# A fused retention, dense and routed-expert kernel: scalings, routing copy and squares moved around the column read, and the order of the last dense units and first expert runs written out

## The chip, the cores and the metric

One core of a Trainium2 chip runs the kernel. The metric is the device time of one execution in microseconds. Five engines work side by side, each through its own queue: TensorE (PE in the profile, its weight loads PEld), VectorE (DVE), ScalarE (ACT), GpSimd (POOL) and SyncE (SP), which here only issues DMAs.

## What is computed

Three layers follow each other on 4608 tokens of 512 values.

```python
# 1: retention, 8 heads of 64, decay per head, sequences of 576
ret = scale * (q @ k^T) * Dmat ;  x = ret @ v
# 2: a dense layer, d_ff = 2048
h = x @ w_in ;  g = h - tanh(h) ;  x1 = g @ w_out
# 3: eight experts, top-1 routing by cosine logits of x1
gate, e = softmax / argmax(x1_normed @ emb_normed^T / tau)
out = gate * (relu(x1 @ w1[e]) @ w2[e])
```

## The kernel before

**Tiles and stages.** The tokens are 36 blocks of 128 (retention) and 18 groups of 256 (dense layer). A dense unit is one group with one eighth of d_ff: 144 units, numbered 0 to 143 in the order `seq`. Every 32-bit product is split in a high and a low part, so `mm1` (L480) has 24 matmuls of 256 columns and `mm2` (L548) 12 of 512. Between them one unit goes through `ch_a` (two ACT steps on the PSUM result h), `ch_c` (two ACT steps), `ch_u` (two DVE steps, the first of them, L518, frees h), `ch_e` (one ACT step, L527), `ch_f` (two DVE steps, L531 and L532, the second waits for L527), `ch_g` (the high part, ACT) and `ch_k` (the low part, DVE, L546). The h tiles have two PSUM buffers.

**Retention of one block.** `att_load` brings q, k, v, n (SP). `scale_q` and `scale_v` (L333, L337) scale q and v on DVE, in place. `b_pe` and `d_pe` (PE) form scores and state updates, `d_ev` and `b_ev` read them on DVE. `c_inter` (PE) puts the part that comes from earlier states in P, for one half of the array; `c_fence` (L432) then reads one column of P on DVE, and only behind that read may `c_pe` (PE) add the rest into the same P. `c_hi` and `c_lo` read P out as x. This read is called the column read.

**Routing of one group**, once its eight units are done: `r1_copy` copies x1 from PSUM (x1p) on DVE, `r1_sq` forms the squares on ACT, `r1_out` stores x1 (SP), `r1_norm` takes the root on POOL; then four small steps `route_2` to `route_5` find expert, gate and place, and `r5_out` writes them in a table in DRAM by indirect DMA (POOL). x1p has two PSUM buffers, both in use by one group.

**Experts.** A run is one expert with two or three tiles of 128 table rows. `b_rec` (L869) reads table rows (SP), `b_gather` (L877) fetches x1 of these tokens (POOL), `b_tr_pe` transposes (PE, L898), `b_tr_hi`/`b_tr_lo` split. `load_w` (L833) brings an eighth of an expert's weights (SP, two buffers of tag "ret"), `split_hi` and `split_lo` split it. `b_mm1`, `b_hi`, `b_lo`, `b_mm2` compute, `b_out` scatters.

**Order.** The schedule is manual: what is emitted first stands first in its engine's queue. Three texts follow each other: START (units 0 to 31 with the retention of blocks 0 to 9 and the splitting of the dense weights, which come as 64-bit words), the loop of `step` (units 32 to 135), and TURN (units 136 to 143 with the first two expert runs, each of two tiles). After them the loop of `b_step` runs the other experts. Before TURN, `early_shift`, `b_rec(0)` and `b_rec(1)` are emitted.

The letters in the texts, each with a number of a unit, block, group, weight piece or run: M `mm1`, N `mm2`, a c u e f g k the steps `ch_`; lq lk lv ln loads, sq sv scalings, B b D d `b_pe` to `d_ev`, I F C `c_inter`, `c_fence`, `c_pe`, xh xl `c_hi`, `c_lo`; R1a copy, R1b squares, R1c store, R1p norm, R2p to R5p the routing's PE steps, R2e to R5e, R2f and R5a its others, R5i the table write; L r R p o q h l the dense weights' load and splitting; W `load_w`, X Y its split, Z `b_rec`, G gather, T U V transposes and their split, P E H Q O the steps of an expert run. A ".V" or ".A" puts the step on DVE or ACT.

In `step(pos)` the block's steps come once in four units (pos % 4 == 2), `route_1` once in eight (pos % 8 == 2), the scalings at pos % 4 == 1, the loads at pos % 4 == 3. So every second column read meets a routing copy.

Of the kernel before, what the change touches and what calls it, by code (L numbers as in the profile page):

```python
# [34 lines left out]
M.136 M.137 a.136 c.136 a.137 c.137 W.0 e.135 f.135 X.0.V Y.0 G.4 G.5 G.0 G.1 u.136 W.1 W.2 X.1.V M.138 g.135 a.138  # L35
c.138 M.139 u.137 Y.1 k.135 N.134 W.3 e.136 f.136 N.135 X.2 Y.2 e.137 X.3 Y.3 f.137 g.137 k.137 g.136 k.136 a.139
c.139 M.140 u.138 R1a.16 R2p.16 M.141 R1b.16 a.140 c.140 u.139 W.4 W.5 e.139 X.4.V Y.4 e.138 f.138 g.138 k.138 u.140
X.5 T.4 f.139 M.142 R2e.16 R3p.16 R3e.16 W.6 N.136 a.141 c.141 R1c.16 R1p.16 e.140 Y.5 X.6 f.140 u.141 R4p.16 g.139
M.143 a.142 c.142 u.142 Y.6 e.142 N.137 N.138 W.7 T.0 W.8 X.8.V X.7 k.139 N.139 Y.7 a.143 c.143 g.140 f.142 g.142
u.143 R2f.16 e.141 Y.8 k.140 N.140 f.141 g.141 W.9 X.9 k.141 k.142 U.0 W.10 Y.9 N.141 W.11 T.1 X.10 Y.10 R4e.16  # L40
R5p.16 e.143 R5a.16 U.1 f.143 g.143 k.143 W.12 V.0 V.1 R5e.16 R5i.16 X.11.V Y.11 N.142 N.143 R1a.17 X.12 U.4 P.0 P.1
E.0 H.0 R2p.17 T.5 P.2 V.4 R1b.17 R1c.17 R1p.17 R2e.17 R3p.17 R3e.17 U.5 Q.0 E.2 H.2 Y.12 R4p.17 W.13 W.14 E.1 H.1
P.3 P.4 R2f.17 R4e.17 R5a.17 E.3.V X.13.V R5p.17 R5e.17 R5i.17 Y.13 H.3 Q.1 Q.2 W.15 Z.2 G.8 E.4 H.4 P.5 P.6 E.6.V
H.6 Q.3 Q.4 E.5.V H.5 P.7 Q.5 V.5 P.8 E.8 H.8 X.15 E.7.V H.7 Q.6 P.9 P.10 E.9.V H.9 P.11 G.9 Q.7 Q.8 Y.15 E.11 H.11
# [11 lines left out]
h.9 f.1 L.11 h.6 l.9 a.2 l.6 g.1 h.7 k.1 a.3 u.2 c.2 u.3 M.4 p.11 d.4 l.7 e.2 c.3 o.10 M.5 b.4 a.4 f.2 e.3 N.1 c.4  # L56
f.3 g.2 u.4 g.3 r.11 k.3 M.6 e.4 k.2 p.10 o.11 a.5 f.4 N.2 a.6 q.11 c.5 u.6 N.3 h.11 u.5 c.6 q.10 e.5 M.7 o.8 h.10
f.5 e.6 g.4 M.8 l.10 g.5 k.4 q.8 a.7 N.4 k.5 h.8 L.13 f.6 a.8 l.8 g.6 N.5 c.8 u.8 c.7 k.6 u.7 M.9 e.8 p.13 f.8 e.7
eg.0 N.6 g.8 l.11 a.9 f.7 r.13 M.10 u.9 g.7 c.9 k.7 k.8 e.9 o.13 N.7 a.10 f.9 c.10 u.10 I.4 g.9 M.11 F.4 e.10 q.13
f.10 h.13 C.4 a.11 l.13 M.12 lq.5 g.10 L.12 u.11 L.14 c.11 lv.5 k.10 N.8 e.11 k.9 a.12 sq.5 f.11 c.12 M.13 u.12 g.11  # L60
r.12 p.12.V k.11 e.12 N.9 o.12 a.13 f.12 c.13 M.14 u.13 p.14 r.14 sv.5 q.12 e.13 M.15 xh.4 o.14 h.12 xl.4 g.12 q.14
B.5 l.12 h.14 D.5 lk.6 lv.6 d.5 N.10 L.15 l.14 b.5 N.11 f.13 k.12 g.13.V I.5 a.14 sv.6 N.12 F.5 r.15 k.13 u.14 p.15
C.5 c.14 o.15 N.13 lq.6 q.15 xh.5 lk.8 e.14 xl.5 h.15 f.14 M.16 a.15 sq.6 g.14 u.15 c.15 B.6 l.15 M.17 e.15 lq.7
k.14 f.15 a.16 N.14 c.16 u.16 g.15.V e.16 sq.7 M.18 k.15 f.16 a.17 R1a.0 c.17 D.6 N.15 u.17 lk.7 g.16 R1c.0 R1b.0
d.6 e.17 R1p.0 M.19 R1a.1.A k.16 R2f.0 a.18 b.6 R1c.1 f.17 R1b.1 R2p.1 N.16 u.18 c.18 R1p.1 g.17.V R2f.1 R2e.1 k.17
R2p.0 e.18 I.6 a.19 f.18 N.17 R2e.0 F.6 u.19 c.19 B.7 g.18 C.6 lv.7 e.19 k.18 M.20 lq.8 f.19 xh.6 za.0 lk.9 xl.6
g.19 sv.7 N.18 k.19 sq.8 a.20 zb.0 c.20 D.7 u.20 zc.0 R3p.0 lv.8 R3p.1 d.7 e.20 N.19 R3e.1 b.7 sv.8 R4p.1 f.20 M.21
R4e.1 g.20 k.20 R5a.1 I.7 a.21 R3e.0 M.22 F.7 c.21 u.21 e.21 N.20 a.22 f.21 c.22 u.22 R4p.0 C.7 g.21.V e.22 R4e.0
M.23 xh.7 lq.10 ln.8 k.21 R5a.0 xl.7 f.22 N.21 a.23 sq.10 g.22 u.23 c.23 R5p.0 B.8 k.22 e.23 M.24 R5e.0 ln.9 f.23
R5i.0 D.8 a.24 N.22 d.8 lv.9 g.23 u.24 c.24 k.23 I.8 e.24 b.8 N.23 f.24 sv.9 g.24 F.8 R5p.1 k.24 M.25 R1a.2 R5e.1  # L70
R1b.2 R1c.2 C.8 M.26 a.25 R5i.1 lq.9 lk.10 xh.8 u.25 c.25 R1p.2 xl.8 R2p.2 a.26 sq.9 M.27 R2f.2 R2e.2 u.26 e.25 c.26
R3p.2 f.25 M.28 e.26 R3e.2 g.25.V f.26 R4p.2 k.25 g.26 B.9 R4e.2 a.27 N.24 ln.10 k.26 c.27 u.27 R5a.2 a.28 R5p.2 D.9
R5e.2 M.29 lv.11 e.27 c.28 u.28 R5i.2 d.9 e.28 N.25 f.28 f.27 I.9 N.26 g.28.V g.27 F.9 k.28 k.27 b.9 a.29 M.30 c.29
u.29 e.29 B.10 a.30 N.27 f.29 lv.10 c.30 u.30 g.29 M.31 e.30 sv.10 k.29 f.30 D.10 a.31 N.28 d.10 lk.11 g.30 c.31
# [1143 lines left out]
```

## Time and profile before

| | us |
|---|---|
| median of three runs | 1516.23 |
| lowest, highest | 1512.62, 1518.34 |
| the profiled execution | 1515.88 |
| its span in the trace | 1514.1 |
| PE busy in the span | 1428.7 (94%) |
| DVE busy | 955.8 (63%) |
| ACT busy | 777.2 (51%) |

The span is what the trace shows from the first instruction to the last. Busy time of PE is the time with at least one matmul under way; ends of matmuls are modelled, so neighbouring groups overlap a little. "Idle before" is the time an engine stood still, with the engine and tile that ended it.

### The profile page before, as it was taken

Reading aid. Unit: us, or ns where it says so; the run is one execution under the profiler, and the core shown is the slowest. Engines: PE = TensorE matmul, PEld = TensorE weight load, DVE = VectorE, ACT = ScalarE, POOL = GpSimd, SP = SyncE. Lnnn points to the kernel's source line nnn. Section 1 sums busy time; section 2 is a strip of 40 time slices with the busy share of each in tenths; the row PEclk is TensorE's granted clock in tenths of the full one; section 3 lists DMA queues with packets and bytes.
Section 4 is the critical chain, followed back from the end, with each engine's and each line's share of the span. In section 5 each row is a group of like instructions: output and inputs, shape, how many; then the busy total and the mean of one; then the engine's idle time right before and its main releaser. Section 6 shows DMA issues by size and latency. Waiting matters only on the chain. (4 is left out here: it accounts for less than half of the span.)

```text
span 1514.1 us, 30499 instructions
## 1 busy us (share of the span) xinstructions
PE 1428.7 (94%) x12696; PEld 1281.9 (85%) x12696; DVE 955.8 (63%) x1910; ACT 777.2 (51%) x1364; POOL 141.5 (9%) x140
## 2 busy tenths in 40 slices
...
GB/s 354 155 28 127 82 57 43 43 98 29 70 43 31 69 43 71 30 43 71 29 69 45 38 62 15 69 99 112 80 121 72 155 96 104 146 81 124 120 42 33
DMA packets 69517, 121.25 MB, mean 80 GB/s; under 512 B 9714, under 2 KB 26482, under 8 KB 69378
## 3 DMA queue, kind: packets, MB, share of 16 engines
...
## 5 line engine op out<-in xcount | busy, mean ns | idle before, releaser
L491 PEld LDWEIGHTS h<-x,w_i 128*128 128x128 f32 x3456 | 426.4, 192 | 32.1 <-issue 15.2
L491 PE MATMUL h<-x,w_i 128*128 128x256 f32 x3456 | 433.4, 282 | 19.2 <-DVE w L518 16.8
L561 PE MATMUL x1p<-w_o,g 128*128 128x512 f32 x1728 | 433.1, 400 | 1.7 <-ACT g L178 1.0
L561 PEld LDWEIGHTS x1p<-w_o,g 128*128 128x128 f32 x1728 | 317.0, 190 | 73.7 <-issue 6.2
L928 PE MATMUL bh<-bx,e 128*128 128x256 f32 (+1 forms) x1536 | 241.9, 307 | 0.8 <-DVE bg L948 0.8
L928 PEld LDWEIGHTS bh<-bx,e 128*128 128x128 f32 x1536 | 231.6, 188 | 10.8 <-DVE bg L948 1.2
L962 PE MATMUL bo<-e,bg 128*128 128x512 f32 x912 | 231.5, 396 | 0.0
L508 ACT ACTIVATE w<-h 128x512 f32<-128x512 f32 x144 | 85.8, 596 | 278.3 <-PE h L491 274.3
L948 DVE SCALAR_TENSOR_TENSOR bg<-bh,bg 128x384 fp32r<-128x384 f32 (+1 forms) x120 | 59.3, 495 | 238.8 <-ACT bg L942 228.8
L942 ACT ACTIVATE bg<-bh 128x384 fp32r<-128x384 f32 (+1 forms) x114 | 50.5, 444 | 286.6 <-PE bh L928 263.4
L962 PEld LDWEIGHTS bo<-e,bg 128*128 128x128 f32 x912 | 165.5, 188 | 29.1 <-issue 0.4
L518 DVE TENSOR_TENSOR w<-h,w 128x512 f32<-128x512 f32 x144 | 99.3, 690 | 115.7 <-ACT w L509 113.2
L532 DVE COPY_PREDICATED w<-w 128x512 f32<-128x512 int32 x144 | 109.0, 757 | 35.7 <-ACT w L527 22.6
L546 DVE TENSOR_TENSOR g<-w,g 128x512 fp32r<-128x512 f32 x144 | 98.9, 690 | 46.0 <-ACT g L178 46.0
L514 ACT ACTIVATE w<-w,nbias 128x512 f32<-128x512 f32 x144 | 104.3, 725 | 4.7
L724 POOL DMA_INDIRECT table<-rec,posi x36 | 45.4, 1260 | 656.3 <-DVE acc L718 601.6
L527 ACT ACTIVATE w<-w,nbias 128x512 f32<-128x512 f32 x144 | 102.8, 715 | 7.1 <-DVE w L519 6.8
L513 ACT ACTIVATE w<-w,nbias 128x512 f32<-128x512 f32 x144 | 104.4, 725 | 0.0
L519 DVE TENSOR_TENSOR w<-w 128x512 f32<-128x512 f32 x144 | 99.7, 692 | 4.9
L178 ACT ACTIVATE g<-w 128x512 fp32r<-128x512 f32 x138 | 85.1, 618 | 30.5 <-DVE w L532 22.5
L531 DVE SCALAR_TENSOR_TENSOR w<-w 128x512 f32<-128x512 f32 x144 | 98.5, 684 | 0.2
L851 DVE TENSOR_TENSOR e<-wr,e 128x1024 fp32r<-128x1024 f32 x64 | 78.3, 1224 | 21.4 <-ACT e L178 21.2
(150 smaller groups left out, 1183.6 us busy)
## 6 DMA issues: line engine op xcount, KB each, us to landing
...
```

What stands on the lines that cost most here:

```text
L491: nc.tensor.matmul(o, lhsT=w[:, c, f * 128 : f * 128 + 128], rhs=x[:, c, :], start=j == 0, stop=j == 11)
L513: nc.scalar.activation(p, u, AF.Square, bias=nbias[:, 1:2])
L514: nc.scalar.activation(p, p, AF.Square, bias=nbias[:, 2:3], scale=RK)
L518: nc.vector.tensor_tensor(b, hps.pop(n), t, op=ALU.subtract)
L519: nc.vector.tensor_tensor(t, t, u, op=ALU.mult)
L527: nc.scalar.activation(u, u, AF.Relu, bias=nbias[:, 0:1])
L531: nc.vector.scalar_tensor_tensor(p, p, RD, t, op0=ALU.add, op1=ALU.mult)
L532: nc.vector.copy_predicated(p, u.bitcast(I32), b)
L546: eng.tensor_tensor(gl, cws.pop(n), gh.bitcast(F32), op=ALU.subtract)
L561: nc.tensor.matmul(xps[g][t], lhsT=gt[:, c : c + 128], rhs=w[:, f, :], start=u == 0 and f == 0 and j == 0, stop=u == 7 and f == 1 and j == 2,)
L928: nc.tensor.matmul(hp, lhsT=w[:, c, fo : fo + 128], rhs=x[:, c, :], start=j == 0, stop=j == 11)
L962: nc.tensor.matmul(bo[i][j], lhsT=a[:, sl], rhs=w[:, f % 2, :], start=f == 0 and k == 0, stop=f == 7 and k == 2)
```

## The change

In `step`, the scalings move one unit earlier (pos % 4 == 0), the routing copy moves behind the column read and ahead of `chain_a`, and the rest of `route_1` moves behind `c_ev` and the block's other reads. The squares read the copy in SBUF and no longer x1p in PSUM. `early_shift` is split in a PE part (es) and a DVE part (et), now tokens, as are `b_rec(0)` and `b_rec(1)`. The loop ends eight units sooner, and TURN now begins at unit 128. START and TURN are written anew; the new START holds the same steps, one of them (r.15) in its DVE form (R.15), and with another choice of ".V" and ".A".

```diff
-    for pos in range(32, NU - 8):
+    for pos in range(32, NU - 16):
...
-    early_shift()
-    b_rec(0)
-    b_rec(1)
     emit(TURN)
...
     def route_1(g):
-        r1_copy(g)
         r1_sq(g)
...
             copy(eng, w[:, t, :], xps[g][t])
+        xps.pop(g)
...
-            nc.scalar.activation(w[:, 2 + t, :], xps[g][t], AF.Square, accum_out=sm[:, t : t + 1])
-        xps.pop(g)
+            nc.scalar.activation(w[:, 2 + t, :], w[:, t, :], AF.Square, accum_out=sm[:, t : t + 1])
...
     # in step(pos)
-        if ru == 2:
-            route_1(rg)
         if pv is not None:
             chain_b(pv)
...
             c_pe(i)
+        if ru == 2:
+            r1_copy(rg)
         if n is not None:
             chain_a(n)
...
                 b_ev(i + 1)
+        if ru == 2:
+            route_1(rg)
...
-        if pos % 4 == 1 and 3 + pos // 4 < NB:
+        if pos % 4 == 0 and 3 + pos // 4 < NB:
             scale_q(3 + pos // 4)
             scale_v(3 + pos // 4)
```

The new TURN:

```python
TURN = """
sv.35 sq.35 M.128 e.127 f.127 I.34 a.128 N.126 F.34 c.128 g.127.V u.128 B.35 k.127 M.129 e.128 f.128 g.128.V N.127
a.129 k.128 c.129 u.129 M.130 R1a.15.A e.129 R1c.15 R1b.15 N.128 f.129 a.130 g.129.V R1p.15 k.129 D.35 c.130 u.130
M.131 R2f.15 e.130 f.130 N.129 a.131 g.130 u.131 c.131 C.34 k.130 M.132 xh.34 d.35 e.131 xl.34 b.35 R2p.15 f.131
a.132 W.1 I.35 M.133 R2e.15 u.132 c.132 g.131.V F.35 k.131 C.35 e.132 R3p.15 W.0 a.133 f.132 N.130 xh.35 u.133 c.133
M.134 R3e.15 xl.35 g.132 e.133 k.132 f.133 R4p.15 a.134 N.131 R4e.15 g.133 c.134 k.133 M.135 u.134 R5a.15 e.134
f.134 N.132 a.135 g.134 u.135 c.135 R5p.15 M.136 k.134 R5e.15 e.135 N.133 f.135 X.0 R5i.15 a.136 Y.0 g.135 es.0
M.137 u.136 W.2 c.136 et.0 e.136 k.135 N.134 X.1.V a.137 Z.0 f.136 Z.1 c.137 M.138 u.137 G.1 g.136 k.136 G.5 e.137
Y.1 G.4 N.135 a.138 f.137 G.0 W.3 X.2 u.138 c.138 T.1 M.139 Y.2 R1a.16.A g.137.V W.4 e.138 R1c.16 k.137 N.136 R1b.16
f.138 a.139 R1p.16 M.140 R2f.16 g.138 u.139 c.139 k.138 N.137 X.3 a.140 Y.3 X.4 M.141 u.140 W.5 e.139 Y.4 c.140
N.138 f.139 W.6 e.140 X.5.V g.139 k.139 T.0 M.142 f.140 a.141 U.0 X.6.V g.140 u.141 N.139 c.141 V.0 U.1 k.140 e.141
M.143 V.1 a.142 f.141 c.142 u.142 T.5 R2p.16 g.141 Y.6 e.142 P.0 R2e.16 f.142 W.7 T.4 E.0 N.140 k.141 H.0 a.143
U.4.V Y.5 R3p.16 U.5 c.143 N.141 u.143 W.8 g.142 V.5 e.143 k.142 Q.0 f.143 N.142 V.4 g.143.V R3e.16 k.143 R4p.16 P.1
X.7.V R4e.16 X.8 N.143 E.1 Y.8 R5a.16 R5p.16 H.1 P.2 W.10 R1a.17 Q.1 E.2 R5e.16 R1c.17 R1b.17 P.3 H.2 R1p.17 R2p.17
Y.7 E.3 R5i.16 P.4 R2e.17 R2f.17 W.9 H.3 Q.2 E.4.V H.4 R3p.17 P.5 R3e.17 X.9 R4p.17 E.5.V P.6 R4e.17 X.10 Q.3 H.5
R5a.17 Y.9 P.7 E.6.V W.11 Q.4 Y.10 R5p.17 H.6 W.12 Q.5 R5e.17 P.8 X.11 E.7.V R5i.17 Q.6 H.7 E.8 Y.11 X.12 P.9 H.8
W.13 Y.12 Q.7 E.9.V W.14 P.10 O.0 H.9 Q.8 E.10 X.13 Z.2 H.10 P.11 Y.13 X.14 Q.9 G.8 E.11.V W.15 Y.14 G.10 P.12 G.9
H.11 Q.10 E.12 H.12 P.13 X.15.V T.8 Y.15 P.14 U.8 E.13.V T.10 V.8 Q.11 H.13 U.10.V P.15 V.10 E.14 H.14 Q.12 T.9
E.15.V Q.13 U.9.V H.15 V.9
"""
```

The head of START, old and new (lines cut where the first dense units are under way):

```diff
-y.0 y.1 y.2 y.3 y.4 y.5 lq.0 lq.2 lq.1 L.0 lq.3 lv.4 lq.4 sq.0 lv.0 lk.0 sq.2 ln.0 L.1 sq.1 lv.1 ln.1 lk.1 L.2 ln.7
-ln.2 lk.2 lv.2 R.0 p.0 ea.0 o.0 lk.3 lv.3 sq.3 L.4 sv.4 lk.4 L.3 q.0 ln.4 ln.5 B.0 sv.0 ln.3 h.0 L.5 sq.4 D.0 l.0
-d.0 b.0 I.0 r.1 F.0 sv.1 C.0 p.1 o.1 xh.0 B.1 q.1 D.1 xl.0 h.1 L.6 d.1 p.2 l.1 I.1 r.2 F.1 b.1 o.2 B.2 eb.0 C.1 sv.2
-ec.0 q.2 xh.1 D.2 d.2 h.2 L.7 l.2 r.4 b.2 ed.0 I.2 p.4 F.2 xl.1 C.2 sv.3 B.3 xh.2 o.4 M.0 p.3 xl.2 r.3 q.4 ef.0 o.3
-a.0 D.3 L.9 d.3 h.4 c.0 q.3 p.5 b.3 L.8 h.3 u.0 I.3 r.5 l.4 e.0 F.3 r.6 f.0 C.3 p.6 l.3 g.0 xh.3 o.5 p.7 xl.3 r.7
-q.5 M.1 o.7 h.5 L.10 p.9 k.0 B.4 l.5 a.1 N.0 ln.6 q.7 r.9 u.1 p.8 M.2 r.8 o.9 c.1 o.6 D.4 q.9 r.10 M.3 lk.5 e.1 q.6
+y.0 y.1 y.2 y.3 y.4 y.5 lq.0 lq.1 L.0 lq.3 lq.2 L.2 L.1 sq.0 lv.0 ln.0 sq.1 lv.5 lk.0 lk.1 lv.1 L.3 lv.4 lk.5 R.0
+p.0 ln.1 lk.9 o.0 lv.3 ln.3 lk.2 sq.3 ln.2 q.0 lv.2 ea.0 sq.2 h.0 L.5 lk.3 lk.4 l.0 r.2 lq.4 p.2 o.2 q.2 r.1 L.7
+sv.0 h.2 o.1 p.1 l.2 B.0 q.1 D.0 d.0 h.1 L.6 sv.1 I.0 b.0 F.0 B.1 l.1 r.3 C.0 sv.5 xh.0 sv.4 p.3 o.3 D.1 xl.0 d.1
+q.3 I.1 F.1 h.3 L.8 b.1 sv.3 C.1 eb.0 sv.2 ec.0 B.2 xh.1 l.3 D.2 xl.1 d.2 M.0 r.5 p.5 ed.0 b.2 ef.0 a.0 sq.4 I.2
+eg.0 o.5 B.3 c.0 D.3 F.2 q.5 C.2 r.7 d.3 L.10 xh.2 p.7 xl.2 h.5 b.3 I.3 o.7 r.6 l.5 p.6 F.3 q.7 C.3 r.8 B.4 u.0 xh.3
+ln.4 h.7 L.4 xl.3 o.8 e.0 M.1 p.10 l.7 r.10 f.0 p.8 D.4 M.2 lq.5 d.4 a.1 q.8 g.0 u.1 L.13 c.1 I.4 b.4 M.3 h.8 sq.5
...
```

## Rows read from the trace of the kernel before

**Rows 1.** Stages: from:to, length, busy us of PE, PEld, DVE, ACT, POOL, clock, DMA.

```profile
0.00:57.50 57.50, 31.49 (x580) 28.83 (x581) 42.78 (x80) 28.65 (x37) 0.77 (x5) 0.69 0.83 304
57.50:257.50 200.00, 197.71 (x1941) 174.95 (x1941) 178.09 (x338) 145.39 (x240) 9.77 (x9) 0.99 0.24 73
257.50:908.50 651.00, 625.27 (x6669) 560.67 (x6668) 480.04 (x1039) 382.35 (x707) 37.57 (x35) 0.99 0.16 52
908.50:1088.50 180.00, 156.99 (x1158) 139.17 (x1157) 114.22 (x241) 83.28 (x150) 24.03 (x22) 0.95 0.24 78
1088.50:1514.00 425.50, 417.24 (x2354) 378.30 (x2352) 140.66 (x214) 137.50 (x231) 69.37 (x69) 1.00 0.30 98
```

**Rows 2.** Waits of PE, 257.5 to 908.5: waiter, releaser, us, times, longest.

```profile
PE P L413 <- DVE fence L436: 25.4, 24, 1.7
```

**Rows 3.** Waits of PE, 908.5 to 1088.5.

```profile
PE h L491 <- DVE w L518: 14.7, 4, 8.9
```

**Rows 4.** Timeline 430 to 446: start, us, instructions, [idle before, releaser].

```profile
432.62 2.99 PE L491 MATMUL h<-x,w_i 128*128 128x256 f32 x24
...
433.67 0.69 DVE L335 TENSOR_TENSOR q<-q,cq 128x512 f32<-128x512 f32 x1
...
434.87 1.28 DVE L180 COPY rt<-x1p 128x512 f32<-128x512 f32 x2
435.54 0.46 PE L413 MATMUL P<-q,S 64*64 64x64 f32 x16
...
435.65 0.60 ACT L588 ACTIVATE rt<-x1p 128x512 f32<-128x512 f32 x1 [2.62 <-DVE rt L180]
...
436.29 0.64 PE L374 MATMUL A<-v,n 64*64 64x64 f32 x16
...
436.81 0.72 ACT L527 ACTIVATE w<-w,nbias 128x512 f32<-128x512 f32 x1
...
438.18 0.34 DVE L436 COPY fence<-P 64x1 f32<-64x1 f32 x2
...
438.38 0.59 PE L413 MATMUL P<-q,S 64*64 64x64 f32 x13 [1.45 <-DVE fence L436]
...
439.87 4.12 PE L561 MATMUL x1p<-w_o,g 128*128 128x512 f32 x12
```

**Rows 5.** Timeline of PE, around a read without routing copy.

```profile
410.52 0.65 PE L374 MATMUL A<-v,n 64*64 64x64 f32 x32
411.79 0.59 PE L413 MATMUL P<-q,S 64*64 64x64 f32 x13 [0.62 <-DVE fence L436]
...
412.84 3.03 PE L561 MATMUL x1p<-w_o,g 128*128 128x512 f32 x12
```

**Rows 6.** DMA engines' busy tenths in 40 slices of 408 to 425.

```profile
DMA  0000000104929699975300000000000000000000
```

**Rows 7.** Timeline 940 to 1022, all engines, around the stall in TURN.

```profile
965.15 0.35 DVE L718 TENSOR_TENSOR acc<-acc,ohb 128x8 bf16<-128x8 bf16 x2
...
972.77 0.81 SPq L873 DMA_DIRECT2D brec<-table  x2
...
976.27 0.99 POOL L879 DMA_INDIRECT xr<-x1d,brec  x1 [5.43 <-issue]
...
977.48 0.69 DVE L180 CAST e<-wr 128x1024 fp32r<-128x1024 f32 x1 [2.33 <-DMA wr<-in_w]
...
980.18 7.94 PE L491 MATMUL h<-x,w_i 128*128 128x256 f32 x48 [8.89 <-DVE w L518]
```

**Rows 8.** Timeline of PE, 880 to 1080: first and last slowed group.

```profile
926.58 4.61 PE L561 MATMUL x1p<-w_o,g 128*128 128x512 f32 x12
...
1005.98 4.33 PE L491 MATMUL h<-x,w_i 128*128 128x256 f32 x24 [2.47 <-DVE w L518]
```

**Rows 9.** Timeline 1320 to 1330: a gather and the transpose that waits for it.

```profile
1324.49 0.98 POOL L879 DMA_INDIRECT xr<-x1d,brec  x1 [0.30 <-PE bh L928]
...
1328.44 0.66 PE L898 MATMUL btp<-ident,xr 128*128 128x128 f32 x4 [0.89 <-DMA xr<-x1d,brec]
```

More of the change, by code (lines that the diff above doesn't have):

```diff
@@ L34 @@
 TURN = """
[L35 to L44, printed above, removed]
@@ L45 @@
-G.10 P.12 Q.9 O.0 E.10 H.10 X.14.V Y.14 E.12 H.12 Q.10 P.13 E.13 H.13 T.8 T.9 U.8.V V.8 Q.11 P.14 U.9.V T.10 U.10
-P.15 V.10 V.9 E.15.V Q.12 Q.13 H.15 E.14 H.14
+sv.35 sq.35 M.128 e.127 f.127 I.34 a.128 N.126 F.34 c.128 g.127.V u.128 B.35 k.127 M.129 e.128 f.128 g.128.V N.127
+a.129 k.128 c.129 u.129 M.130 R1a.15.A e.129 R1c.15 R1b.15 N.128 f.129 a.130 g.129.V R1p.15 k.129 D.35 c.130 u.130
+M.131 R2f.15 e.130 f.130 N.129 a.131 g.130 u.131 c.131 C.34 k.130 M.132 xh.34 d.35 e.131 xl.34 b.35 R2p.15 f.131
@@ L55 @@
-q.5 M.1 o.7 h.5 L.10 p.9 k.0 B.4 l.5 a.1 N.0 ln.6 q.7 r.9 u.1 p.8 M.2 r.8 o.9 c.1 o.6 D.4 q.9 r.10 M.3 lk.5 e.1 q.6
[L56 to L74, printed above, removed]
@@ L75 @@
-u.31 C.9 k.30 N.29 xh.9 ln.11 b.10 lq.11 xl.9
+y.0 y.1 y.2 y.3 y.4 y.5 lq.0 lq.1 L.0 lq.3 lq.2 L.2 L.1 sq.0 lv.0 ln.0 sq.1 lv.5 lk.0 lk.1 lv.1 L.3 lv.4 lk.5 R.0
+p.0 ln.1 lk.9 o.0 lv.3 ln.3 lk.2 sq.3 ln.2 q.0 lv.2 ea.0 sq.2 h.0 L.5 lk.3 lk.4 l.0 r.2 lq.4 p.2 o.2 q.2 r.1 L.7
+sv.0 h.2 o.1 p.1 l.2 B.0 q.1 D.0 d.0 h.1 L.6 sv.1 I.0 b.0 F.0 B.1 l.1 r.3 C.0 sv.5 xh.0 sv.4 p.3 o.3 D.1 xl.0 d.1
+q.3 I.1 F.1 h.3 L.8 b.1 sv.3 C.1 eb.0 sv.2 ec.0 B.2 xh.1 l.3 D.2 xl.1 d.2 M.0 r.5 p.5 ed.0 b.2 ef.0 a.0 sq.4 I.2
```

29 lines of the change are left out of this document (27 added, 2 removed).

## The prediction, made before the changed kernel ran

> **What bounds the kernel now.** I read the span cut into its five stages first [rows 1]. The reader is to look at the TensorE (PE) column: from 57.5 us on PE is busy in nearly all of the span, so the time is PE's matmul time plus PE's idle time plus what a lowered clock costs. Idle are 26.0 us in the opening (57.5 - 31.49), 2.3 in the rest of START (200.00 - 197.71), 25.7 in the loop of `step` (651.00 - 625.27), 23.0 in the stretch of TURN (180.00 - 156.99) and 8.3 in the experts (425.50 - 417.24). VectorE (DVE) is busy for 480 of 651 us in the loop and 114 of 180 in TURN: its order matters there, not its sum.
>
> Second, who PE waited for. In the loop it is one thing: 25.4 us in 24 waits for the column read (`c_fence`, L436) [rows 2], so the whole idle time of that stage. In TURN the largest is 14.7 us in 4 waits for `ch_u` (L518), the longest 8.9 [rows 3].
>
> Third, the timeline around one read [rows 4]. PE has issued `c_inter`, `b_pe` and `d_pe`, and may go on with `c_pe` only when DVE has read the column. P is there from about 436.0 (435.54 + 0.46). The read starts at 438.18, because in DVE's queue these stand ahead of it: both scalings (1.2 us, from 433.67 to 434.87), the routing copy (1.28), then `ch_f`; and the second half of `ch_f` also waits for the ACT step of L527, which is queued behind the two squares of the routing (435.65 on). PE stands idle for 1.45 us. In units without routing copy the wait is 0.62 [rows 5]. Twelve reads of each kind make the 24.
>
> **Part 1, the loop: scalings one unit earlier, copy behind the read, squares from SBUF.** Without scalings and copy, DVE ends `ch_k` of the unit before at 433.7, and `ch_f` needs 0.7 + 0.75. Its L527 is now behind nothing on ACT, since the squares come after `c_hi`. So `ch_f` ends at about 435.2, before P is there, and the read runs at 436.0 + 0.15 to 436.5. PE is busy with `d_pe` until 436.9 [rows 4]. The wait goes, with some 0.4 us of slack. In the other kind the scalings' 1.2 us alone exceed the 0.62 us of waiting [rows 5], so it goes too. What it is worth: the 25.4 us of idle time [rows 2], plus the overlap that groups of matmuls have where nothing stands between them (in rows 4 `c_inter` starts 0.07 before the modelled end of the group ahead, elsewhere up to 0.2): 0.1 to 0.2 x 24 = 2 to 5 us. [...] In all 25.4 + 3.5 + 2.3 = 31 us; I take 30, since a tenth may stay here and there.
>
> What the moved steps cost where they go. Scalings: 1.2 us of DVE at the end of a unit, ahead of the next `ch_f`; in rows 4 DVE ran the same steps without making anyone but PE's read wait, and PE is 5.8 us per unit, so they are hidden as long as q and v have landed. Their loads are issued four at a time, and the DMA engines are idle again 8.5 us after 408, at 416.5 [rows 6]; the scaling would start near 428. On the other parity the loads go out at about 437 to 440, and the scaling starts two units later, past 455. Over 10 us of slack on both: cost zero. Copy: behind the read it ends near 437.8. It holds `ch_u` of this unit back by 1.28 us, which frees the PSUM tile of a matmul two units later (over 10 us away): zero. It also frees the x1p banks for the `mm2` that follows `c_pe`; without the wait `c_pe` ends at about 438.2, so 0.4 us of slack, and a cost between 0 and 0.4 x 12 = 5 us if that estimate is off by as much again. I take zero, as the row has the copy complete first. The stores of x1 on SP's queue wait for the copy, and the loads of the next block stand behind them: about 2 us later, out of the 10.
>
> Squares: ACT's square from PSUM takes 0.60, an ACT step of the same size from SBUF 0.72 [rows 4]: 36 x 0.12 = 4.3 us more on an engine that is busy for 382 of 651 us [rows 1], not on the path. [...]
>
> **Part 2, TURN: the last 16 units and first expert runs, 908.5 to 1088.5.** Now: b_rec(0) and b_rec(1) stand on SP's queue ahead of the first weight load. They wait for the routing table: L718 ends at 965.50, brec goes out at 972.77 [rows 7], the weight load behind it. DVE's queue has the split of that weight (X.0.V) ahead of `ch_u`; it starts at 977.48, after waiting for the transfer. Only then does L518 free the h tile, and PE goes on at 980.18 after 8.89 idle [rows 7]. The new text issues W.1 and W.0 in units 132 to 133; between W.0 and X.0 PE has M.134, M.135, M.136 and N.130 to N.133, some 20 us, and Z.0 and Z.1 are behind them. So this stall goes. What else is idle in TURN (23.0 - 8.9 = 14.1) comes from DVE working off its backlog after it. Three groups also ran slowed: 926.58 (4.61 against 3.03) [rows 5, 8], 980.18 (7.94 for two `mm1`, 2 x 2.9 = 5.8 at full clock) [rows 7] and 1005.98 (4.33 against 2.92) [rows 4, 8]: 1.6 + 2.1 + 1.4 = 5.1. At most 23.0 + 5.1 = 28 us are to be had.
>
> Where new waits can come: PE works down its queue, and the transposes T.1 and T.8 of gathered rows stand in it at fixed places. From the last routing step on DVE (965.50) to the first gather on POOL (976.27) it took 10.8 us [rows 7], from a gather's issue to the matmul that waited for it 3.95 (1324.49 to 1328.44) [rows 9]: 14.7 us. In the new text PE has three `mm1` and three `mm2` between R5p.15 and T.1: 3 x (2.92 + 2.9) [rows 4, 5], 17.0 to 17.8 us; DVE ends R5e.15 some 2.3 us after R5p.15 (end of `ch_u`, `ch_k`, then 11 small steps, 1.9): 17.0 against 17.4, a wait of 0 to 1. Ahead of T.8 stand six P and six Q of 1.4 each (half an `mm1` or `mm2` [rows 4, 5]), 16.8 us, against 2 + 14.7 = 16.7, or more where the weight loads fill the queues: 0 to 3. DVE's list for TURN (from M.128) sums to some 119 us over 147 of PE, so no engine is full. I take 4 us for all new waits (0 to 15): TURN gives 28 - 4 = 24, between 13 and 28.
>
> **Part 3, START.** PE starves only in the first 57.5 us, where DVE is the queue that ends last before M.0 to M.4. Summing DVE's steps by the new and old order, ahead of M.0 stand 31.3 against 31.4 us, ahead of M.1 47.5 against 46.9, ahead of M.4 63.0 against 64.4, ahead of M.16 138.2 against 141.7: about equal. The transfers move: the last load that block 1 needs (ln.1) has 7.25 MB up to and with it instead of 5.0, so at 304 GB/s [rows 1] it lands some 7 us later; DVE has decode work in between. From -4 to +7, I take 0. Nothing of the expert loop changes, nor the tail: 0.
>
> **Sum.** The profiled run took 1515.88 with a span of 1514.1; its distance to the median of 1516.23 is nothing here. 1515.9 - 30 - 24 - 0 = 1462 us.
>
> **Rivals.**
> (a) TURN trades one stall for others. If only the 8.89 and its slow group go (11), the time is 1515.9 - 30 - 11 = 1475, with worse 1480 to 1486. For it: DVE's 119 of 147 is dense, and 16 weight loads have two buffers. Against: each split has a unit or more of distance to its load. Chance 0.17.
> (b) START loses: all of the 7 us of ln.1 reach M.0, as PE has nothing else before it: 1469; if the 2.3 us of the later START double, 1471. Chance 0.13.
> (c) The read stays late in one of the two kinds (`ch_f` still ending after P): half of the loop's 30 is lost, 1477. Against it are the 0.4 us and more of slack worked out above. Chance 0.07.
> (d) Slower: the scaling one unit earlier meets q and v that have not landed; DVE's queue then stops, with `ch_f` and the read behind it, in 24 units. It begins to cost where the landing comes more than 10 us later than in rows 6, and outweighs the 54 us of gain from 10 + 54/24 = 12.3 us on; by 3 us beyond that the time is 1516 + 3 x 24 - 0 = 1588. Nothing in rows 6 hints at this. Chance 0.02.
> (e) The change does not reorder what I think: queues keep the order of the text only if DVE's list follows it, which rows 4 show (scaling, scaling, copy, `ch_f`, read). Then 1516. Chance 0.02.
>
> **How the numbers follow.** The forecast 1462 has chance 0.59, its own bounds being 1451 (START 4 better, no new waits, 3 more of overlap) and 1472. Cases (a) to (c) end at 1469 to 1486. The range 1452 to 1480 leaves out (d), (e), the worse half of (a) and little at the lower end. A measurement of this kernel can tell about 0.5% (7.6 us) from no change: faster by more than that is the forecast and (a) to (c), 0.96; within it (e), 0.02; slower (d), 0.02.
>
> **What would show it.** Loop: no row of the waits for L436, 24 blocks each about 1.2 us shorter, read before the end of `d_pe`, no slowed `mm2` behind it. If there is a wait of x1p for L180, the copy is the new bound. TURN: no wait over 3 us for L518, brec behind the first weight loads, small waits at most at the transposes (L898) for gathered rows. START: M.0 within some 4 us of before. Wrong would be the forecast if PE's idle time in 908.5 to 1060 stayed over 15 us, or the loop's over 5.

## The result, and the profile after

The changed kernel takes 1452.51 us (median, 1451.74 to 1453.25), the kernel before 1514.42 beside it: a ratio of 0.9595 (95% interval 0.956 to 0.963), 61 us less (0.0405 x 1515). The forecast of 1462 was 9.5 us too slow; the time lies in its range of 1452 to 1480, but only 0.5 us above the lower end. The profiled run took 1453.25 with a span of 1451.1 us.

The span by the same stages as [rows 1], cut at the same places of the program (M.32, M.128, first group of the third expert run; the first cut, inside START, lies near M.1 and is not the same to the microsecond); columns as there: length, busy time of PE, PEld, DVE, ACT and POOL, granted clock, DMA share, GB/s.

```profile
0.00:54.50 54.50, 29.78 (x604) 27.93 (x604) 41.08 (x78) 26.44 (x34) 1.08 (x5) 0.71 0.79 285
54.50:254.80 200.30, 197.08 (x1925) 172.59 (x1918) 181.28 (x345) 145.23 (x240) 10.34 (x9) 0.99 0.27 82
255.10:868.08 612.98, 612.98 (x6670) 552.99 (x6669) 480.50 (x1037) 382.84 (x708) 38.83 (x35) 1.00 0.17 55
868.08:1024.98 156.90, 152.52 (x1158) 135.11 (x1156) 114.03 (x244) 83.57 (x147) 24.55 (x22) 0.99 0.28 90
1024.98:1451.10 426.12, 417.41 (x2354) 378.44 (x2352) 141.02 (x215) 137.62 (x231) 69.39 (x69) 1.00 0.29 98
```

Cut in the same way, the kernel before has 257.5, 651.1, 179.9 and 425.6 us for START, loop, TURN and experts; now they take 255.1, 613.0, 156.9 and 426.1. So START gave 2.4 us, the loop 38.1, TURN 23.0, the experts -0.5: 63.0 in the two profiled spans. Forecast were 0, 30, 24 and 0. In the loop PE is now busy in every microsecond; its busy time fell as well, from 625.3 to 613.0. That second fall, 12.3 us, is what the forecast had too small: it had booked 4.6 for it (30 - 25.4).

The timeline of a read with routing copy, PE, DVE and ACT, against [rows 4]:

```profile
269.21 0.46 PE L419 MATMUL P<-q,S 64*64 64x64 f32 x16
269.74 0.34 DVE L442 COPY fence<-P 64x1 f32<-64x1 f32 x2 [0.85 <-PE P L419]
269.96 0.65 PE L380 MATMUL A<-v,n 64*64 64x64 f32 x32
270.11 1.29 DVE L186 COPY rt<-x1p 128x512 f32<-128x512 f32 x2
270.43 0.41 PE L419 MATMUL P<-q,S 64*64 64x64 f32 x16
270.66 0.65 PE L419 MATMUL P<-ret,v 64*64 64x64 f32 x32
271.24 3.03 PE L567 MATMUL x1p<-w_o,g 128*128 128x512 f32 x12
272.72 0.63 ACT L594 ACTIVATE rt<-rt 128x512 f32<-128x512 f32 x1
```

DVE now waits for PE (0.85), not PE for DVE. The read ends at 270.08, `c_pe` starts at 270.43, 0.18 us ahead of the modelled end of `d_pe` (269.96 + 0.65 = 270.61), and `mm2` follows. The copy of both x1p banks ends at 271.40, 0.16 us behind the start of `mm2`, yet `mm2` does not wait: by the program's order it writes the first bank first, and half of the copy is done near 270.8.

In TURN one row of waits is left where [rows 3] stood, in two places, T.1 and T.8, the transposes of gathered rows:

```profile
PE btp L908 <- DMA xr<-x1d,brec: 4.4, 2, 3.3
...
934.48 0.66 PE L908 MATMUL btp<-ident,xr 128*128 128x128 f32 x4 [1.12 <-DMA xr<-x1d,brec]
...
1015.13 0.63 PE L908 MATMUL btp<-ident,xr 128*128 128x128 f32 x4 [3.27 <-DMA xr<-x1d,brec]
1015.51 2.62 PE L938 MATMUL bh<-bx,e 128*128 128x256 f32 x12
```

The group behind T.8 took 2.62; its like takes 1.55, so 1.07 us were lost there.

### The profile page after: what moved, and what is told of

Its sections match the earlier page's. It is cut to its first block, busy times and chain, and to the rows that moved or that the text cites. A ratio compares the mean times of both kernels' runs of the same rounds, so it can differ in the third digit from the quotient of the medians.

```text
span 1451.1 us, 30509 instructions
## 1 busy us (share of the span) xinstructions
PE 1410.1 (97%) x12696; PEld 1267.3 (87%) x12696; DVE 958.2 (66%) x1916; ACT 776.0 (53%) x1358; POOL 144.2 (10%) x140
## 3 DMA queue, kind: packets, MB, share of 16 engines
q1 hardware_dynamic: 61826, 99.32, 20.8%
## 5 line engine op out<-in xcount | busy, mean ns | idle before, releaser
L497 PEld LDWEIGHTS h<-x,w_i 128*128 128x128 f32 x3456 | 421.8, 190 | 15.8 <-DVE w L524 4.4
L497 PE MATMUL h<-x,w_i 128*128 128x256 f32 x3456 | 429.1, 281 | 2.9 <-DVE w L524 2.9
L514 ACT ACTIVATE w<-h 128x512 f32<-128x512 f32 x144 | 85.9, 597 | 259.7 <-PE h L497 254.3
L515 ACT ACTIVATE w<-h 128x512 f32<-128x512 f32 x144 | 85.5, 594 | 0.0
```

The costliest lines, as they stand in the source:

```text
L497: nc.tensor.matmul(o, lhsT=w[:, c, f * 128 : f * 128 + 128], rhs=x[:, c, :], start=j == 0, stop=j == 11)
```

## The experiments

Theory A: the loop's gain is larger than its idle rows because a wait of TensorE costs a fixed amount beyond the idle time shown. Theory B: the loop gave what was forecast, and the rest came from START or TURN. The first three kernels behind the changed one in the table have one part of the change each. Every ratio is to the kernel before, measured beside that kernel; its medians there run from 1513.3 to 1517.9, so rows are to be compared by their ratios.

| kernel | us, median | ratio to before (95%) |
|---|---|---|
| changed | 1452.51 | 0.9595 (0.956 to 0.963) |
| loop only | 1478.57 | 0.9756 (0.9739 to 0.9772) |
| TURN only | 1495.03 | 0.9863 (0.9847 to 0.9880) |
| START only | 1512.15 | 0.9981 (0.9970 to 0.9992) |
| scalings only | 1485.50 | 0.9807 (0.9790 to 0.9823) |
| copy and squares only | 1493.34 | 0.9847 (0.9826 to 0.9868) |
| changed, 3 reads | 1468.26 | 0.9679 (0.9661 to 0.9696) |
| changed, 5 reads | 1483.51 | 0.9776 (0.9760 to 0.9792) |
| changed, squares from PSUM | 1498.53 | 0.9876 (0.9859 to 0.9893) |
| before, first weights ahead | 1515.66 | 0.9992 (0.9977 to 1.0007) |
| before, one line of TURN | 1512.53 | 0.9980 (0.9961 to 0.9998) |
| before, both of these | 1513.16 | 0.9998 (0.9983 to 1.0013) |
| changed, transposes later | 1447.00 | 0.9544 (0.9526 to 0.9561) |

**The loop alone.**

```diff
-        if pos % 4 == 1 and 3 + pos // 4 < NB:
+        if pos % 4 == 0 and 3 + pos // 4 < NB:
...
-        if ru == 2:
-            route_1(rg)
...
             c_pe(i)
+        if ru == 2:
+            r1_copy(rg)
...
+        if ru == 2:
+            route_1(rg)
...
-            nc.scalar.activation(w[:, 2 + t, :], xps[g][t], AF.Square, accum_out=sm[:, t : t + 1])
+            nc.scalar.activation(w[:, 2 + t, :], w[:, t, :], AF.Square, accum_out=sm[:, t : t + 1])
```

> The kernel before with part 1 alone (scalings one unit earlier, copy behind the column read, squares from SBUF; old START, old TURN). Theory A, that a wait of TensorE costs more than the idle time shown for it (about 0.42 us more each, since the overlap at the end of the group ahead and the quick start of the group behind are lost): 25.4 + 24 x 0.42 + 2.3 = 38 us faster, about 1478. Theory B, that the loop's gain is the idle time with 3.5 us of overlap and the slowed groups, and the rest of the 38 us seen between the two traces comes from the new START or TURN: 28 to 31 us faster, about 1486. The PE waits for the column read are gone from the loop in both.

A ratio of 0.9756 is 37 us (0.0244 x 1515, by the interval 34.5 to 39.5). That is theory A; the 28 to 31 of theory B lie outside. No PE wait for the read is left in the loop.

**TURN alone, START alone.** In the first of these the squares of groups 15 to 17, whose steps TURN holds, read SBUF too (`early_shift` and the two `b_rec` are tokens there, as in the change).

```diff
-TURN = """ ...
+TURN = """ ...
-    for pos in range(32, NU - 8):
+    for pos in range(32, NU - 16):
...
-            nc.scalar.activation(w[:, 2 + t, :], xps[g][t], AF.Square, accum_out=sm[:, t : t + 1])
+            nc.scalar.activation(w[:, 2 + t, :], xps[g][t] if g < 15 else w[:, t, :], AF.Square, accum_out=sm[:, t : t + 1])
```

> The kernel before with part 2 alone: the new order of the last 16 units and the first expert runs, old START and old loop body (squares of groups 15 to 17 from SBUF, the others from PSUM as before). If the gains are separate, TURN gives 23 us (20 to 26), about 1492. If the dense order of the new TURN only works because the new loop hands over an earlier VectorE, it gives 10 to 15 us and shows waits for ch_u (L518) or the column read again.

```diff
-START = """ ...
+START = """ ...
```

> The kernel before with part 3 alone: the new order of START. By the stage table of the two traces 2.4 us faster (M.0 2.5 us earlier), about 1513; by the prediction's term 0, by its rival (b) 7 us slower, with ln.1 landing later.

TURN alone gives 20.8 us (0.0137 x 1515, by the interval 18.2 to 23.2; the stage in the trace gave 23.0), START 2.9 (1.2 to 4.5). The three parts sum to 0.0400, the whole change to 0.0405: the gains are separate.

**The two moves of the loop, one at a time.**

```diff
-        if pos % 4 == 1 and 3 + pos // 4 < NB:
+        if pos % 4 == 0 and 3 + pos // 4 < NB:
```

> Of part 1 only the scalings are moved (pos % 4 == 0); routing copy and squares as before. In the 12 units without routing copy the wait for the column read goes (0.62 each, the scalings' 1.2 us exceed it). In the 12 with it 1.45 - 1.2 = 0.25 us stays. By theory A (0.42 more per wait that goes) 12 x (0.62 + 0.42) + 12 x 1.2 + 2.3 = 29 us faster, about 1487, with some 3 us of idle time left in the loop; by theory B 12 x 0.62 + 12 x 1.2 + 2.3 = 24. If the squares on ScalarE's queue hold ch_f's second half as late as now, the waits with copy stay at 1.4 and the gain is 12 us.

For the next one the copy and the squares are moved as above and the scalings stay.

> Of part 1 only the routing copy is moved behind the column read and the squares read SBUF; scalings in their old place. All 24 reads then are of the kind without copy: 24 waits of about 0.6 us, 14 to 16 us of idle time left of 25.4. Theory A and B agree on the waits that only get shorter: 12 x 0.83 + 2.3 (the two slowed mm2) = 12 us faster, about 1504.

Waits of PE in the loop, scalings only first, then copy and squares only:

```profile
PE P L413 <- DVE fence L436: 4.1, 13, 0.4
```

```profile
PE P L413 <- DVE fence L436: 7.6, 12, 0.8
```

(Of the 13 waits of the first, 12 are behind units 32 to 127.) Scalings alone: 29 us (26.8 to 31.8), as theory A had it and not the 24 of theory B; the 12 reads without copy are on time and those with copy wait 0.25 to 0.44. Copy alone: 23 us (20.0 to 26.4) instead of 12. That expectation was wrong: only the 12 reads without copy still wait (0.62 in most), the others do not wait at all. What DVE does ahead of the two kinds differs by more than the copy; this is DVE's queue in the kernel before, ahead of a read of the kind without copy:

```profile
408.66 0.17 DVE L675 TENSOR_TENSOR sm<-cf,sm 128x16 f32<-128x16 f32 x1
408.87 0.17 DVE L677 CAST ohb<-sm 128x16 bf16<-128x16 f32 x1
408.98 0.69 DVE L335 TENSOR_TENSOR q<-q,cq 128x512 f32<-128x512 f32 x1
409.59 0.68 DVE L339 TENSOR_TENSOR v<-v,cf 128x512 f32<-128x512 f32 x1
410.19 0.68 DVE L531 SCALAR_TENSOR_TENSOR w<-w 128x512 f32<-128x512 f32 x1
410.98 0.73 DVE L532 COPY_PREDICATED w<-w 128x512 f32<-128x512 int32 x1
411.61 0.33 DVE L436 COPY fence<-P 64x1 f32<-64x1 f32 x2
```

The routing steps of `route_4e` (eight of 0.17 us) stand there as well. By the order of the queue this kind was late by routing steps and scalings, the other by scalings and copy (with the squares ahead of L527). Moving the scalings alone puts the first kind on time, moving the copy with the squares alone the second; the routing steps were not moved by themselves.

**What a wait costs.** The changed kernel with the read repeated, three and five times in all:

```diff
-    def c_fence(i):
-        for c in range(2):
+    def c_fence(i, k=1):
+        for c in (0, 1) * k:
...
-            c_fence(i)
+            c_fence(i, 3)
```

> The changed kernel with the column read done three times instead of once (4 more reads of 0.17 us ahead of c_pe in most of the 24 blocks of the loop, 0.66 us). In the changed kernel the read ends some 0.3 us before c_pe starts, so PE waits about 0.3 us 24 times, 7 us of idle time. Theory A (a wait costs its idle time and 0.42 more): 24 x 0.72 = 17 us slower than the changed kernel, about 1470. Theory B (idle time and at most 0.15 of overlap): 7 to 11 us slower, about 1461.

> The same with the column read done five times (8 more reads, 1.33 us). PE waits about 1.0 us 24 times, 23 us of idle time by the trace. Theory A: 24 x 1.42 = 34 us slower than the changed kernel, about 1487, so that time lost less idle time is the same 10 us as with three reads: a fixed price for each wait. Theory B: 23 to 27, about 1478. If the surplus grows with the length of the wait it is no fixed price but the lowered clock behind it, and the groups behind show it.

Three reads, waits of PE in the loop, then the timeline of one read (PE):

```profile
PE P L419 <- DVE fence L442: 1.5, 9, 0.2
...
296.19 0.65 PE L380 MATMUL A<-v,n 64*64 64x64 f32 x32
297.00 0.59 PE L419 MATMUL P<-q,S 64*64 64x64 f32 x13 [0.16 <-DVE fence L442]
...
298.05 3.04 PE L567 MATMUL x1p<-w_o,g 128*128 128x512 f32 x12
```

Five reads:

```profile
PE P L419 <- DVE fence L442: 17.3, 22, 0.9
...
298.84 0.59 PE L419 MATMUL P<-q,S 64*64 64x64 f32 x13 [0.91 <-DVE fence L442]
...
299.89 1.43 PE L567 MATMUL x1p<-w_o,g 128*128 128x512 f32 x5
```

Three reads cost 12.7 us by the ratios (0.0084 x 1515), five 27 (0.0181 x 1515), both known to some 6 us only, since the changed kernel's own ratio is. Both expectations had the waits too long (0.3 and 1.0 us; they are 0.08 to 0.18 and 0.84 to 0.92, and shorter or none in the five blocks told of below), so these totals decide nothing: 12.7 lies between the theories, 27 at theory B's upper end. What decides is the loss beyond the idle time. With three, the list of waits shows 1.5 us of idle time: nearly all of the loss is in no idle row. From M.32 to M.128 the trace with five reads is 26.5 us longer than that of the changed kernel (639.5 against 613.0), with 17.3 in the list of waits: 9.2 us beyond it, near theory A's 10. The profiles let it be measured read by read: the step from the start of `c_inter` to the start of `mm2` lasts 2.03 us in the changed kernel, where nothing waits (269.21 to 271.24 above).

| read | idle row | step | lost | lost beyond idle |
|---|---|---|---|---|
| before, with copy | 1.44 | 3.88 | 1.85 | 0.41 |
| before, without copy | 0.62 | 3.06 | 1.03 | 0.41 |
| scalings only, with copy | 0.26 | 2.70 | 0.67 | 0.41 |
| 3 reads, with copy | 0.08 | 2.53 | 0.50 | 0.42 |
| 3 reads, without copy | 0.16 | 2.61 | 0.58 | 0.42 |
| 5 reads, with copy | 0.84 | 3.28 | 1.25 | 0.41 |
| 5 reads, without copy | 0.91 | 3.36 | 1.33 | 0.42 |
| before, edge block, without copy | 0.62 | 2.84 | 0.89 | 0.27 |
| before, edge block, with copy | 1.73 | 3.96 | 2.01 | 0.28 |
| 5 reads, edge block | 0.16 | 2.38 | 0.43 | 0.27 |

An edge block is one in which a sequence begins: that half has no earlier state, `c_inter` has 8 matmuls instead of 16, and the step without a wait is 1.95 us in the changed kernel (346.75 to 348.70). The loop has five of them among its 24 reads. The 0.08 is no row: it is `c_pe`'s start less the modelled end of `d_pe` (269.99 - 269.91), too short for the waits' list. The surplus is 0.41 us in 19 blocks and 0.27 in the five edge blocks, at any length of the wait, so theory A holds in kind: a fixed price, though not the same for each block. The lowered clock is not its cause: the granted clock of a `c_pe` behind a wait, in the trace with five reads, is 1.00, and the `mm2` groups behind these reads take 2.86 to 2.89 from their start to that of the next group, but for two in the kernel before. Columns as in the stages:

```profile
298.80:299.90 1.10, 1.06 (x49) 0.98 (x49) 1.01 (x3) 0.81 (x2) 0.00 (x0) 1.00 0.88 328
```

The 0.41 has two halves. With a wait, `c_pe` takes 1.05 us to the start of `mm2` (297.00 to 298.05, 298.84 to 299.89, and [rows 5]); without one 0.81 (270.43 to 271.24): 0.24. The other 0.17 is the overlap of `c_pe` with `d_pe`, which is modelled to end at 270.61 when `c_pe` is already running from 270.43.

The stretch from the transposes of routing group 3 to those of group 14, 88 units with 22 of the reads, gives the same sum. It takes 596.5 us before, 561.8 in the changed kernel, 562.0 with the loop alone, 571.5 with three reads and 585.7 with five. Three reads: 9.8 us, 0.44 a read. Before: 34.8 us, 1.58 a read, of which 1.06 is idle time, 0.38 surplus (17 x 0.41 + 5 x 0.27 = 8.3) and 0.14 the two slowed places (0.4 us of `c_pe` and 1.1 to 1.2 of `mm2` in each, 3.1 in all).

**Squares from PSUM.** The changed kernel with the squares' old source in their new place:

```diff
-            nc.scalar.activation(w[:, 2 + t, :], w[:, t, :], AF.Square, accum_out=sm[:, t : t + 1])
+            nc.scalar.activation(w[:, 2 + t, :], xps[g][t], AF.Square, accum_out=sm[:, t : t + 1])
```

> The changed kernel with the squares reading PSUM again, in their new place behind c_hi. Theory: copy behind the read is only free because the squares have left PSUM; now the x1p banks come free when the squares end (273.9 in the trace of the changed kernel) and not when the copy ends (271.4), and mm2 starts at 271.2: it waits some 2.2 us in 12 units, with the price of a wait and slowed groups 12 x 2.6 to 3.5 = 31 to 42 us slower than the changed kernel, about 1488. Rival: mm2 of the next group goes to other banks and nothing is late, within 3 us of the changed kernel.

It is 43 us slower than the changed kernel (0.0281 x 1515), at the upper end of the 31 to 42 expected. Waits of PE in the loop, one `mm2` behind such a wait, and the windows of 269.8 to 271.4 and of 271.4 to 274.4 around it (columns as in the stages):

```profile
PE x1p L567 <- ACT rt L593: 26.0, 12, 2.2
...
269.82 4.73 PE L567 MATMUL x1p<-w_o,g 128*128 128x512 f32 x12 [2.15 <-ACT rt L593]
...
269.80:271.40 1.60, 1.58 (x5) 1.12 (x6) 1.53 (x5) 1.16 (x3) 0.72 (x1) 0.84 0.97 303
271.40:274.40 3.00, 3.00 (x9) 2.31 (x8) 2.66 (x6) 0.00 (x0) 0.00 (x0) 0.52 0.53 189
```

`mm2` of the next group waits 2.15 us for the squares, 12 times, and 10 of the 12 groups then ran slowed; the one shown had a granted clock of 0.52 for 3 us. From `c_inter` to the start of `mm2` it is 4.25 us here: 2.03 + 2.15 + 0.07. So the 43 us are 26.0 of waits, some 16.3 of ten slowed groups (4.4 to 4.6 us to the next group instead of 2.86) and 0.8 of surplus. These waits, ahead of 128x512 matmuls, cost their idle time and mostly a slowed group; the 0.41 was seen only between the small 64x64 groups.

**TURN's long wait.** The prediction put the 8.89 us of [rows 7] down to the queue of weight loads. One edit of the kernel before moves those loads:

```diff
+    load_w(0, 0)
+    load_w(0, 1)
     early_shift()
     b_rec(0)
     b_rec(1)
...
-M.136 M.137 a.136 c.136 a.137 c.137 W.0 e.135 f.135 X.0.V Y.0 G.4 G.5 G.0 G.1 u.136 W.1 W.2 ...
+M.136 M.137 a.136 c.136 a.137 c.137 e.135 f.135 X.0.V Y.0 G.4 G.5 G.0 G.1 u.136 W.2 ...
```

> The kernel before with one edit in TURN: the loads W.0 and W.1 are issued ahead of early_shift, b_rec(0) and b_rec(1), so they no longer stand behind the wait for the routing table. If that queue is the cause of the 8.89 us wait for ch_u, the wait goes with the slowed mm1 behind it (2.1): 9 to 11 us faster, about 1505. If VectorE's backlog holds ch_u anyhow, a wait of 5 us or more stays in its place and the gain is 0 to 4 us.

It gave nothing clear of the noise (0.9977 to 1.0007, so 3.5 us at most), the expectation's second case. The timeline around the wait, PE and DVE (here and below a group at the end of a window is cut there):

```profile
966.50 7.32 PE L491 MATMUL h<-x,w_i 128*128 128x256 f32 x48
...
976.94 0.73 DVE L532 COPY_PREDICATED w<-w 128x512 f32<-128x512 int32 x1 [9.09 <-ACT w L527]
977.57 0.68 DVE L180 CAST e<-wr 128x1024 fp32r<-128x1024 f32 x1
...
980.25 3.11 PE L491 MATMUL h<-x,w_i 128*128 128x256 f32 x13 [6.44 <-DVE w L518]
```

The split no longer waits for its load, but DVE has stood 9.09 us for ScalarE's L527, and PE still stands 6.44; the pair of `mm1` ahead (7.32) ran slowed here, 5.70 in the trace of before, which takes back 1.6 of the 2.45 us that the wait is shorter. The trace of before had such a wait of DVE too, and the prediction did not look at it; the second row is PE's next wait there:

```profile
974.42 0.73 DVE L532 COPY_PREDICATED w<-w 128x512 f32<-128x512 int32 x1 [7.47 <-ACT w L527]
...
996.39 2.98 PE L491 MATMUL h<-x,w_i 128*128 128x256 f32 x24 [2.77 <-DVE w L518]
```

In the text, `e.135` (L527) stands behind `a.137` and `c.137`, which need M.137: ScalarE must wait for two `mm1` before it may end the unit ahead. So the next kernel mends that line and leaves the loads, and the one behind it has both edits.

```diff
-M.136 M.137 a.136 c.136 a.137 c.137 W.0 e.135 f.135 X.0.V Y.0 G.4 G.5 G.0 G.1 u.136 W.1 ...
+M.136 a.136 c.136 e.135 f.135 u.136 M.137 a.137 c.137 W.0 X.0.V Y.0 G.4 G.5 G.0 G.1 W.1 ...
```

> The kernel before with one line of TURN in another order and the queue of the weight loads left as it was: e.135, f.135 and u.136 stand ahead of M.137, a.137 and c.137, so ScalarE's L527 for unit 135 no longer stands behind the tanh steps of unit 137, and ch_u of 136 no longer behind the split of the first weight. With the loads moved up (the kernel that showed no gain) VectorE still sat 9.1 us behind L527. Theory: this order is the cause of the 8.9 us wait; it shrinks to some 1.4 us (ch_f from 971.2, ch_u to 972.6, PE ready at 971.3), 7 to 10 us faster, about 1507. Rival: the backlog of splits meets the next units, the waits of 2.8 and 2.5 us behind it grow by as much, 0 to 3 us faster.

> Both single edits of TURN together in the kernel before: W.0 and W.1 issued ahead of the routing records, and e.135, f.135 and u.136 ahead of M.137. Alone the first gave nothing and the second 3 us: with the order mended, VectorE stood 2.2 us for the weight behind the records, and PE 3.2 us for ch_u of 137 behind that. Theory (two causes in series, each covering the other): together the 3.2 us and the slowed group behind it (1.6) go as well, 3 + 4.8 = 8 us faster, about 1508. Rival (the new order gains because the whole list of splits is spread out): the waits move on to the next units, 3 to 4 us faster as with the order alone, about 1512.

PE's waits with the one line:

```profile
971.00 2.99 PE L491 MATMUL h<-x,w_i 128*128 128x256 f32 x24 [1.47 <-DVE w L518]
977.18 4.57 PE L491 MATMUL h<-x,w_i 128*128 128x256 f32 x24 [3.19 <-DVE w L518]
```

And with both:

```profile
973.31 7.44 PE L491 MATMUL h<-x,w_i 128*128 128x256 f32 x48 [1.78 <-DVE w L518]
...
990.87 1.53 PE L491 MATMUL h<-x,w_i 128*128 128x256 f32 x8 [4.61 <-DVE w L518]
```

With the one line the 8.89 us became 1.47 and 3.19 with a slowed group (4.57) behind, 3.0 us faster (0.3 to 5.9): the first case expected (7 to 10) was wrong, and its rival (0 to 3) held. With both edits it is 1.78, but the next wait, 2.77 before, became 4.61 with a slowed group (4.60) behind it, and the time is that of before (0.9983 to 1.0013). Both numbers expected there, 8 us and 3 to 4, were too large; the rival's mechanism is what the trace shows: from M.136 to the next pair of `mm2` 7.6 us are won (14.8 us instead of 22.4), and 3.5 of them are lost again at the next wait. The work that DVE has behind the stall meets the next units. From the transposes of group 14 to those of group 17 the profiles have 166.5 us before, 164.5 with the loads moved, 165.4 with the one line, 162.4 with both, 145.7 with the new TURN alone and 144.4 in the changed kernel. The 4 us that this single profile has with both edits do not show in the timed runs (at most 2.6). Only the whole new order gives the 20 us. Which of its other moves carry them was not tried one by one and stays open.

**The two waits that the new TURN keeps.** The changed kernel with three transposes later in PE's queue:

```diff
-... u.138 c.138 T.1 M.139 Y.2 ...
+... u.138 c.138 M.139 T.1 Y.2 ...
-X.15.V T.8 Y.15 P.14 U.8 E.13.V T.10 V.8 Q.11 H.13 U.10.V P.15 V.10 E.14 H.14 Q.12 T.9 ...
+X.15.V Y.15 P.14 E.13.V H.13 Q.11 P.15 T.8 U.8 E.14 H.14 V.8 T.10 U.10.V V.10 Q.12 T.9 ...
```

> The changed kernel with three transposes of gathered rows later in TensorE's queue: T.1 behind M.139, T.8 and T.10 behind Q.11 and P.15. In the changed kernel PE waits 1.12 us at T.1 and 3.27 at T.8, and the group behind the second ran 1.07 us slower. Theory A: all of it goes, with 2 x 0.4 for the waits themselves: 4 to 6 us faster than the changed kernel, about 1447.5. Rival: the split of the last gathered rows (V.9) now ends late and the first group of run 2 waits for it as long, within 1.5 us of the changed kernel.

It takes 1447.00 us (1445.75 to 1448.93), 5.5 less than the changed kernel, as expected, and the ratios' intervals (0.9526 to 0.9561 against 0.956 to 0.963) barely touch; in the traces the stage from M.128 on takes 151.2 us against 156.9. In TURN PE waits for one thing:

```profile
PE bh L938 <- DVE bx L186: 0.4, 1, 0.4
```

The 4.4 us of waits and the slowed 1.07 add up to what was gained; the 2 x 0.4 that the expectation added for the waits themselves cannot be told from noise here.

## Why the prediction was right, and where it was off

**The loop: mechanism right, size too small by 8 us.** The read is on time in both kinds, as worked out (the one shown starts 0.07 us behind the modelled end of `c_inter`, 269.74 against 269.67, where the prediction's estimate was 0.15), and PE's idle time is 0 of 25.4. The step that failed is the term "the overlap that groups of matmuls have where nothing stands between them", 0.1 to 0.2 for each wait, 3.5 us. It counted one half of what a wait costs. The second half, a `c_pe` that takes 1.05 instead of 0.81, stood in [rows 5] (411.79 to 412.84) and could not be seen without a read that is on time, for which the trace of before has no row in the loop. Measured, the term is 19 x 0.41 + 5 x 0.27 = 9.1 us instead of 3.5. The 2.3 us in the sum are what the `mm2` of the two slowed places lost (4.21 and 4.12 us at 330.46 and 439.87 of the trace of before, against 3.03 in [rows 5]). The places came to 3.1, since their `c_pe` ran slowed too (1.41 and 1.49 us to the start of `mm2` instead of 1.05, at a granted clock of 0.70 and 0.66); the granted clock was 0.70 in the 3.9 us of the second's `mm2`.

```profile
439.90:443.80 3.90, 3.90 (x15) 3.15 (x13) 3.42 (x9) 1.63 (x4) 0.00 (x0) 0.70 0.41 139
```

25.4 + 9.1 + 3.1 = 37.6 stands against 38.1 in the trace. The 1 us that was then left off for waits that stay was not needed: none stayed.

**What the moved steps cost: zero, as forecast.** Scalings meet no late transfer: DVE goes into all 24 pairs of the loop and out of them without idle time, one of them below, and the rival with 1588 us has no sign.

```profile
542.48 0.42 DVE L648 COPY rt<-lp 128x256 f32<-128x256 f32 x1
542.81 0.68 DVE L341 TENSOR_TENSOR q<-q,cq 128x512 f32<-128x512 f32 x1
543.41 0.68 DVE L345 TENSOR_TENSOR v<-v,cf 128x512 f32<-128x512 f32 x1
544.01 0.69 DVE L537 SCALAR_TENSOR_TENSOR w<-w 128x512 f32<-128x512 f32 x1
```

The copy costs nothing either, but not by the slack worked out. The forecast set the end of the whole copy 0.4 us ahead of `mm2`; in the trace it ends 0.16 us behind the start of `mm2` (271.40 against 271.24), and only the first bank is free 0.4 us ahead. The sentence also left out a condition: the copy frees the x1p banks only because the squares no longer read them. With the squares on PSUM behind the read the change loses 43 of its 61 us. The prediction had booked the squares' new source as a cost alone.

**The price of the squares' source was sized by the wrong row.** It took 0.72 from L527, an activation with a bias. ScalarE in the loop, squares before (L588) and after (L594), then L527; busy us, mean ns:

```profile
L588 ACT ACTIVATE rt<-x1p 128x512 f32<-128x512 f32 x24 | 14.1, 593 | 31.5 <-DVE rt L180 31.5
```

```profile
L594 ACT ACTIVATE rt<-rt 128x512 f32<-128x512 f32 x24 | 14.9, 627 | 0.0
```

```profile
L527 ACT ACTIVATE w<-w,nbias 128x512 f32<-128x512 f32 x96 | 68.6, 715 | 1.1 <-DVE w L519 1.1
```

From SBUF it is 0.034 us more (627 ns against 593), not 0.12. The end did not depend on it: PE is busy in all of the loop's 612.98 us.

**TURN: size right, cause not.** 24 forecast, 23.0 in the trace and 20.8 alone; PE's idle time fell from 23.0 to 4.4, where the forecast left 4, and its busy time by 4.5, where the forecast had 5.1 of slowed groups. The new waits were placed right and sized nearly so: T.1 0 to 1 forecast and 1.12 measured, T.8 0 to 3 and 3.27. But the early weight loads, from which "this stall goes" was argued, were one cause of several: moved alone they give nothing. The step that failed is the end of the chain, read from the last releaser of DVE (2.33 us for the load) without the 7.47 us ahead of it. That the sum for TURN came out all the same was in part luck: it booked all idle time as gone, and the argument given for that did not carry it. Rival (a) described the single edits, not the change: there one stall was traded for others.

**START: 0 forecast, 2.9 measured**, inside the bounds of -4 to +7. Rival (b) did not come: M.0 starts at 38.0 (40.5 before), of which single profiles tell little (last point below). What in the new order gave the 2.9 us was not tried.

**The sum** with the terms as measured alone: 1515.9 - 37 - 21 - 3 = 1455, against 1452.5. The loop's 8 us and START's 3 went the same way and took the time to the very end of the range.
